# Front of an attention and gated feed-forward kernel: constants, load gates, queue order and the place of the scores

## The chip, the cores and the metric

The kernel runs on one core of one Trainium2 chip. The metric is the device time of one execution in microseconds (us), lower is better. Single-core executions here scatter by about 1 us; faster or slower needs 2%, which is 7.1 us. Every execution also has a mean granted TensorE clock: 1.0 is full speed, and one halved stretch of 3.4 us in some 355 us shows as 0.995. Where in the execution such a stretch lay is recorded for the profiled executions alone.

## The reference, cut to what matters

```
scores = scale * q @ k^T          # batch 8, heads 8, 576 positions, head size 64
mask   = window of 32 (heads 0-3) or 32 positions at stride 4 (heads 4-7), both causal
x      = softmax(scores + mask) @ v            -> 4608 tokens x 512
out    = (gelu(x @ w_gate) * (x @ w_val)) @ w_out      # 512 -> 1536 -> 512
```

All inputs and the output are float32 in HBM; the kernel computes in float16 with float32 sums.

## The kernel before

Tokens go through the feed-forward part in nine chunks of 512 columns. Attention of batch b is worked in between, as far as the next chunk needs it. Only the front has nothing to hide behind: q and k of batch 0 must land, be cast, transposed, scored, exponentiated and multiplied by v, before chunk 0 can start.

Words used below: w is w_gate and w_val together, loaded in thirds, each with a gate part and a value part. xT is the transposed output of attention. The first product multiplies xT by w; its sum over 512 is cut into four k slices, its 1536 result columns into twelve column blocks. The second product is by w_out, the output weights. The denominators are the sums of the softmax, the numerators its products with v. A gate, in the code, makes a DMA wait until another DMA has landed.

The parts that the change touches:

```python
def load_w(i):                      # a third of w_gate and one of w_val, GpSimd's queue (casts to f16)
    both = [nc.gpsimd.dma_start(out=t[i], in_=w[:, cs]...) for t, w in ((wg_t, moe_w_gate), (wv_t, moe_w_val))]
    gated(both[0])                  # waits for the DMA that gate["dma"] names, once
    return both
...
mask_plain()                        # GpSimd; VectorE then makes bias_p of mask_p, first thing after "ones"
gate_v = v_plain(0, sv0, nc.sync)   # five DMAs; the last one is returned
...
warm(30, 7)                         # 30 matmuls of ones, to bring the clock up
for vp_, _, vt_, _ in vset:         # constants, six memsets on VectorE
    nc.vector.memset(...)
for hp in range(2):                 # casts of q (VectorE) and k (ScalarE), batch 0
    ...
gate["dma"] = gate_v
load_w(0)
... scores of four head pairs, denominators ...
load_w(1)
copy("pool", tiles["v", 0][1], r4(first_vd))
wg2, _ = load_w(2)
...
num_split(0, 4)                     # ScalarE copies PSUM to SBUF, GpSimd multiplies into xT[0]
num_split(1, 0)                     # the same into xT[1]
...
gate["dma"] = wg2                   # q, k of batch 1 wait for it
... SyncE loads q, k of batch 1; GpSimd: dilated q, k of batch 1, output weights 0,
    then four casts of q, k, then output weights 1 and 2, dilated v ...
```

In chunk 0 the transposes of the cast q, k of batch 1 follow the column blocks 10 and 11 (`t_plain(1, q61, nb - 10, ...)`). The scores of batch 1 are laid between thirds of the second product (`ffn2`). GpSimd works its list strictly in order, so a DMA that it issues later starts later, and a cast that waits holds up everything behind it.

The softmax here doesn't subtract the row's maximum and nothing guards it: scores larger than these inputs give would overflow.

Of the kernel before, what the change touches and what calls it, by code (L numbers as in the profile page):

```python
# [21 lines left out]
def kernel(  # L22
# [100 lines left out]
    def mask_plain():  # L123
        nc.gpsimd.memset(mask_p, 1.0)
        band(mask_p[:, 0:PB].rearrange("p (r c) -> p r c", c=PW), 0, 0)
        band(mask_p[:, PB : PB + P].rearrange("p (r c) -> p r c", r=1), 0, 0)
        band(mask_p[:, PB + P : PH].rearrange("p (r c) -> p r c", r=1), 0, 64)
        nc.vector.tensor_scalar(bias_p, mask_p, 1.0, 60000.0, ALU.subtract, ALU.mult)

    def mask_dil():  # L130

# [5 lines left out]
    def load_w(i):  # L137
        cs = slice(i * CH, (i + 1) * CH)
        both = [
            nc.gpsimd.dma_start(out=t[i], in_=w[:, cs].rearrange("(kc p) n -> p kc n", p=P))  # L140
            for t, w in ((wg_t, moe_w_gate), (wv_t, moe_w_val))
        ]
        gated(both[0])
        return both
# [9 lines left out]
    def gated(ins):  # L154

        if "dma" in gate:
            tc.add_manual_dep(ins.ins, gate.pop("dma").ins.name, SYNC, reason="order of loads")
# [36 lines left out]
    def v_plain(b, sv, eng):  # L194
        for kb in range(5):
            k0 = min(kb * P, S - P)
            last = eng.dma_start(out=sv[:, kb], in_=v[b, 0:HK, k0 : k0 + P, :].rearrange("h p d -> p h d"))  # L197
            gated(last)
        return last

    def v_cast(b, sv):
        vp, vd, vt, vr = tiles["v", b]
# [37 lines left out]
    def load_v_dil(b):  # L240
        nc.gpsimd.dma_start(out=fl(tiles["v", b][1]), in_=quads(v, b, HK, 0, 4 * P))
        load_v_dil_rest(b)
# [53 lines left out]
    def cast_six(eng, q6, st, t, hp):  # L296

        h = slice(2 * hp, 2 * hp + 2)
        copy(eng, q6[:, t, :, h, :], st[:, t, h, :].rearrange("p h (r d) -> p r h d", r=6))
# [326 lines left out]
    def warm(n, bank):  # L626
        for _ in range(n):
            nc.tensor.matmul(ps[:, bank, :], ones[:, 0:P], ones, start=True, stop=True)


    for t, src, eng in ((0, q, nc.sync), (1, k, nc.scalar)):
        eng.dma_start(out=first_p[:, t], in_=sixes(src, 0))
# [11 lines left out]


    warm(30, 7)
    for vp_, _, vt_, _ in vset:
        nc.vector.memset(vp_.rearrange("p j g x d -> p (j g) x d")[:, :, 1, :], 1.0)
        nc.vector.memset(vt_[:, :, 1, :], 1.0)
    for hp in range(2):  # L650
        for t in range(2):
            cast_six(("dve", "act")[t], q6, first_p, t, hp)
    for hp in range(2):
        t_plain(0, q6, hp, 2 * hp, ("act", "dve"))
    nc.vector.tensor_scalar(bias_d, mask_d, 1.0, 60000.0, ALU.subtract, ALU.mult)
# [25 lines left out]
    t_dil(0, 1, qd0, 6, ("act", "act"))  # L681
    last_keys(0, 0, 2)
    last_keys(0, 2, HK, nc.gpsimd)
    load_w(1)
    copy("pool", tiles["v", 0][1], r4(first_vd))
    wg2, _ = load_w(2)

    dt0, dt1 = (den(n, -2 * n, t.rearrange("p (b c) -> p b c", c=32)) for n, t in enumerate(first_t))
    recip(0, dt0)
# [9 lines left out]
    num(3, 0)  # L699


    gate["dma"] = wg2
    st1 = ldp.tile([R6, 2, HK, 6 * D], F32, tag="st", name="st1")
    for t, src in ((0, q), (1, k)):
        gated(nc.sync.dma_start(out=st1[:, t], in_=sixes(src, 1)))
    sv1 = new_v(1)
    new_qt(1)
    qd1 = load_eights(1)
    load_wo(0)
    q61 = ldp.tile([R6, 2, 6, HK, D], F16, tag="qp", name="qp1")  # L710
    for hp in range(2):
        for t in range(2):
            cast_six("pool", q61, st1, t, hp)
    wo1 = load_wo(1)
    wo2 = load_wo(2)
    gate["dma"] = wo1
    v_plain(1, sv1, nc.sync)
    load_v_dil(1)
    v_cast(1, sv1)
    gate["dma"] = wo2  # L720
    tiles["plain", 2] = load_batch_plain(2)

    mm0 = 0
# [18 lines left out]
    for c in range(NCH):  # L742
        if 1 <= c and c + 2 < B:
            tiles["plain", c + 2] = load_batch_plain(c + 2)
            load_batch_rest(c + 2)
        pv_at = values_a.get(c, {})
        s_list = list(scores.get(c, ()))
        if c < 2:
            pairs = ((2, 3), (0, 1)) if c == 0 else ((0, 1), (2, 3))
        else:  # L750
            pairs = (ends, (mm0 + 1, mm0 + 2))
        SB = 4 - mm0

        masks = []
        pend = None
        for nb in range(NNB):
            if nb == 0 and c < 2:
                ffn1_two(c, ((4, 5), (6, 7)) if c == 0 else ((6, 7), (2, 3)), range(NKC), False)
            elif nb == 0 and late:
                ffn1_two(c, pairs, (2, 3, 0, 1) if c in (2, 3) else range(NKC), True)  # L760
            elif nb > 1 or not (c < 2 or late):
                ffn1(c, nb, pairs[nb % 2])
            if pend is not None:
                (norm_both_x if is_plain(pend) else norm_x)(pend, SB)
                pend = None
            if nb in pv_at:
                pend = pv_at[nb]
                if is_plain(pend):
                    emit_both(pend, SB)
                    norm_both_r(pend, SB)  # L770
                else:
                    emit_pv(pend, SB, wide=True)
                    norm_r(pend, SB, wide=True)
            if c == 0 and nb > 9:
                t_plain(1, q61, nb - 10, 4 + 2 * (nb - 10), ("act", "dve"))
            if nb == NNB - 1 and c > 0 and s_list:
                n = s_list.pop(0)
                masks.append(emit_s(n, SB, pe_mask=n in biased))

        def s_next():  # L780
            if s_list:
                n = s_list.pop(0)
                masks.append(emit_s(n, SB, pe_mask=n in biased))

        def mask_next():
            mask = masks.pop(0) if masks else None
            if mask is not None:
                mask()


        if c == 0:
            load_batch_rest(2)

            def third(i):
                for tb in range(2):
                    ffn2(c, tb, 2 + tb, fcs=range(4 * i, 4 * i + 4))
                    if i == 2:
                        store(c, tb, 2 + tb, "act")

            def s_of(n):  # L800
                mask = emit_s(n, 4, pe_mask=n > 5)
                if mask is not None:
                    masks.append(mask)


            s_of(4)
            t_dil(1, 0, qd1, 2, ("dve", "dve"))
            t_dil(1, 1, qd1, 0, ("dve", "dve"))
            last_keys(1, 0, HK)
            mask_next()  # L810
            third(0)
            s_of(5)
            den(4, -2)
            third(1)
            mask_next()
            s_of(6)
            den(5, -2)
            third(2)
            s_of(7)
            ffn2(c, 2, 2, {3: [lambda: den(6, -2)], 9: [lambda: num(4, 4)]})  # L820
            store(c, 2, 2, "act")
            ffn2(c, 3, 3, {0: [lambda: den(7, -2)], 4: [lambda: num(5, 6)]})
            store(c, 3, 3, "act")
            num(6, 0)
            num(7, 4)
            gelu_table()
        else:
            todo = list(values_b.get(c, ()))
            lone = c in values_b

            ends = (0, 3) if c == 1 else ends
            going = []

            def do(kind, tb):
                if kind == "s":
                    s_next()
                elif kind == "m":
                    mask_next()
                elif kind == "x":
                    norm_x(*going.pop(0))  # L840
                elif kind == "v":
                    n, flip = todo.pop(0), ends[tb % 2] != mm0
                    bank = mm0 + 1 - flip
                    emit_pv(n, bank, flip=flip)
                    norm_r(n, bank, flip=flip)
                    going.append((n, bank, flip))
                else:
                    n = todo.pop(0)
                    emit_pv(n, SB)
                    norm_parts(n, SB, min(S, (c + 2) * CH - n // NHP * S))  # L850

            for tb in range(4):
                at = [(fc, kind) for t, fc, kind in places.get(c, ()) if t == tb]
                hooks = {}
                for fc, kind in at:
                    if fc < NNB:
                        hooks.setdefault(fc, []).append(lambda kind=kind, tb=tb: do(kind, tb))
                bank = ends[tb % 2] if lone else mm0 + tb
                ffn2(c, tb, bank, hooks)
                store(c, tb, bank, "dve" if c > 5 and tb == 3 else "act")  # L860
                for fc, kind in at:
                    if fc == NNB:
                        do(kind, tb)
            if lone:
                gelu_table()

            late = lone and len(values_b[c]) > 2
            if c == 3:
                mm0 = 4 - mm0
            if c == 3 or not lone:  # L870
                ends = (mm0, mm0 + 3)
            while masks:
                mask_next()
# [28 lines left out]
```

## Time and profile before

| | before |
|---|---|
| time, median of 3 runs (lowest, highest) | 356.04 us (355.39, 356.18) |
| span of the profiled execution | 354.9 us, mean clock 0.995 |
| TensorE busy | 339.6 us, 96% |
| first product of chunk 0, its second k slice | 24.18 us, 25.54 us |
| first product of chunk 1 | 68.13 us |

TensorE is the engine with the most work, so its idle time is all that a reordering can win. The table of stretches, the chain of waits and the lists of GpSimd and TensorE are shown in the prediction. GpSimd's list: its columns are start, length, engine, line, operation, count, and in brackets the idle time before and what ended it.

```profile
41.06 0.82 POOL L292 CAST qp<-st 96x768 f16<-96x768 f32 x1 [13.37 <-DMA st<-in_q_dram]
44.18 2.37 POOL L292 CAST qp<-st 96x768 f16<-96x768 f32 x3 [2.30 <-DMA st<-in_k_dram]
```

These are the casts of q, k of batch 1 in the kernel before: GpSimd waits for q until 41.06 and for k until 44.18, so the first cast k is ready at 45.0. TensorE's transposes of them start at 45.33, without a wait, six of q and then six of k:

```profile
45.33 0.68 PE L305 MATMUL ps<-ident,qp 96*128 96x96 f16 x12
```

### The profile page before, as it was taken

Reading aid. Unit: us, or ns where it says so; the run is one execution under the profiler, and the core shown is the slowest. Engines: PE = TensorE matmul, PEld = TensorE weight load, DVE = VectorE, ACT = ScalarE, POOL = GpSimd, SP = SyncE. Lnnn points to the kernel's source line nnn. Section 1 sums busy time; section 2 is a strip of 40 time slices with the busy share of each in tenths; the row PEclk is TensorE's granted clock in tenths of the full one; section 3 lists DMA queues with packets and bytes.
Section 4 is the critical chain, followed back from the end, with each engine's and each line's share of the span. In section 5 each row is a group of like instructions: output and inputs, shape, how many; then the busy total and the mean of one; then the engine's idle time right before and its main releaser. Section 6 shows DMA issues by size and latency. Waiting matters only on the chain.

```text
span 354.9 us, 5997 instructions
## 1 busy us (share of the span) xinstructions
PE 339.6 (96%) x2338; PEld 164.0 (46%) x2338; DVE 201.9 (57%) x307; ACT 147.7 (42%) x219; POOL 81.4 (23%) x121
## 2 busy tenths in 40 slices
PE   8869999999999999999999999999999999999995
PEld 3534454444444444444545454544454444444442
DVE  1793466743486448873778756995499414403320
ACT  1653355343553364535462448235732223323321
POOL 8391161353143153063004400240000000000000
PEclk9998999999999999999999999999999999999999
DMA  8999969999999999799148962791200020020002
GB/s 178 174 197 205 210 98 206 181 155 180 235 175 161 237 162 168 196 173 152 61 125 187 136 125 77 180 172 50 88 2 0 31 89 1 2 81 37 2 30 89
DMA packets 106316, 44.44 MB, mean 125 GB/s; under 512 B 83280, under 2 KB 101584, under 8 KB 106288
## 3 DMA queue, kind: packets, MB, share of 16 engines
q1 hardware_dynamic: 84192, 31.14, 39.1%
q0 software_dynamic: 21696, 12.33, 27.7%
q10 hardware_dynamic: 400, 0.59, 0.7%
q8 instruction: 18, 0.29, 0.4%
q14 instruction: 10, 0.08, 0.1%
HBM read 39.85 MB, written 9.44 MB: 139 GB/s over the span
## 4 chain that ended last, share of the span: by engine, by line
PE 74%; DVE 10%; DMA 6%; issue 3%; POOL 2%; SPq 2%; ACT 1%; DVEq 0%; POOLq 0%; ACTq 0%
PE ps L575 46%; PE ps L609 21%; PE ps L463 4%; DMA sv<-in_v_dram 3%; DMA qTd<-rd 2%; DVE u_all L598 2%; DMA out_dram<-osb 2%; DVE dt L491 2%; DVE xT L501 1%; SPq L197 1%; PE ps L381 1%; DVE P L391 1%; POOL xT L676 1%; DVE qTd L294 1%; PE ps L351 1%
## 5 line engine op out<-in xcount | busy, mean ns | idle before, releaser
L598 DVE SCALAR_TENSOR_TENSOR u_all<-g,ps 128x512 f16<-128x512 f16 x108 | 72.8, 683 | 78.7 <-PE ps L575 71.5
L575 PE MATMUL ps<-xT,wg 128*128 128x512 f16 x432 | 115.0, 382 | 2.2 <-POOL xT L676 1.9
L597 ACT ACTIVATE g<-ps 128x512 f16<-128x512 f32 x108 | 63.9, 596 | 125.1 <-PE ps L575 124.6
L575 PE MATMUL ps<-xT,wv 128*128 128x512 f16 x432 | 114.8, 381 | 0.5 <-ACT osb L620 0.3
L609 PE MATMUL ps<-wo,u_all 128*128 128x512 f16 x432 | 99.8, 380 | 0.1
L575 PEld LDWEIGHTS <-wv 128*128 128x128 f16 x432 | 42.4, 98 | 54.7 <-issue 3.5
L575 PEld LDWEIGHTS <-wg 128*128 128x128 f16 x432 | 41.5, 98 | 49.5 <-issue 2.4
L609 PEld LDWEIGHTS <-u_all 128*128 128x128 f16 x432 | 39.6, 98 | 45.8 <-issue 0.7
L620 ACT ACTIVATE osb<-ps 128x512 f32<-128x512 f32 x33 | 19.7, 597 | 39.7 <-PE ps L609 39.2
L219 POOL CAST qp<-st 128x2048 f16<-128x2048 f32 x6 | 11.4, 1894 | 97.2 <-DMA st<-in_k_dram 57.2
L535 DVE STREAM_TRANSPOSE rb<-rc 128x576 f32<-128x576 f32 (+4 forms) x34 | 25.3, 743 | 1.3
L524 DVE STREAM_TRANSPOSE dt<-ps 128x576 f32<-128x576 f32 x21 | 16.3, 777 | 15.1 <-PE ps L463 15.1
L383 ACT ACTIVATE P<-ps 128x1152 f16<-128x1152 f32 x16 | 18.1, 1130 | 14.2 <-PE ps L381 13.5
L361 ACT ACTIVATE P<-ps 128x960 f16<-128x960 f32 x16 | 15.5, 970 | 12.2 <-PE ps L351 12.2
L550 DVE TENSOR_TENSOR xT<-ps,rb 128x576 f16<-128x576 f32 x16 | 17.9, 1127 | 1.4 <-PE ps L463 1.1
L622 DVE TENSOR_SCALAR osb<-ps 128x512 f32<-128x512 f32 x3 | 2.1, 692 | 27.8 <-PE ps L609 27.8
L463 PE MATMUL ps<-P,ones 128*64 128x96 f16 (+5 forms) x162 | 11.1, 249 | 3.9 <-DVE P L391 2.8
L391 DVE TENSOR_TENSOR P<-P,mask_d 128x1152 f16<-128x1152 f16 x11 | 8.3, 755 | 10.2 <-ACT P L383 10.2
L391 DVE TENSOR_TENSOR P<-P,mask_p 128x1344 f16<-128x1344 f16 x14 | 12.3, 887 | 2.6 <-ACT P L362 2.5
L463 PEld LDWEIGHTS <-ones 128*64 128x64 f16 x162 | 7.2, 108 | 12.7 <-issue 8.1
L491 DVE STREAM_TRANSPOSE dt<-ps 64x576 f32<-64x576 f32 x14 | 10.9, 780 | 0.4
L203 POOL CAST vp<-sv 128x1024 f16<-128x1024 f32 x8 | 8.6, 1076 | 10.5 <-DMA sv<-in_v_dram 10.5
(82 smaller groups left out, 243.9 us busy)
## 6 DMA issues: line engine op xcount, KB each, us to landing
out_dram<-osb SPq DMA_DIRECT2D x36, 256.0 KB, 2.0
sv<-in_v_dram SPq DMA_DIRECT2D x40, 128.0 KB, 3.7
st<-in_q_dram SPq DMA_DIRECT2D x24, 128.0 KB, 4.1
st<-in_k_dram SPq DMA_DIRECT2D x24, 128.0 KB, 3.2
vd<-in_v_dram POOLq DMA_DIRECT2D x7, 256.0 KB, 6.8
wg<-in_moe_w_gate_dram POOLq DMA_DIRECT2D x3, 512.0 KB, 7.6
wv<-in_moe_w_val_dram POOLq DMA_DIRECT2D x3, 512.0 KB, 9.5
wo<-in_moe_w_out_dram POOLq DMA_DIRECT2D x3, 512.0 KB, 8.4
```

Source lines behind the costliest of these rows:

```text
L383: nc.scalar.activation(pt, ps[:, b0 : b0 + 4, 0:DW], AF.Exp, bias=0.0, scale=scale)
L391: nc.vector.tensor_tensor(pt, pt, mb, ALU.mult)
L463: nc.tensor.matmul(o, lhs, rhs, start=st, stop=True, skip_group_check=True)
L491: nc.vector.transpose(dt[64 * hl : 64 * hl + 64].rearrange("p b c -> p (b c)"), both_rows(1 - hl, b0, hl))
L524: nc.vector.transpose(dst, den)
L535: nc.vector.transpose(rb[:, 0 : 32 * nb].rearrange("p (b c) -> p b c", c=32), bass.AP(tensor=rc.tensor, offset=rc.offset, ap=[rc.ap[0], [1 ...
L550: nc.vector.tensor_tensor(dst.rearrange("p (i m s) -> p i m s", m=2, s=2), num, rb.rearrange("p (s m i) -> p i m s", s=2, m=2), ALU.mult,)
L575: nc.tensor.matmul(ps[:, bank, :], w[:, kc, ns], xT[kc][:, tok], start=first, stop=end)
L597: nc.scalar.activation(g, ps[:, banks[0], :], AF.Gelu)
L598: nc.vector.scalar_tensor_tensor(u_all[:, nb, :], g, USCALE, ps[:, banks[1], :], ALU.mult, ALU.mult)
L609: nc.tensor.matmul(ps[:, bank, :], u_all[:, fc, tb * P : (tb + 1) * P], wo_t[fc // 4][:, fc % 4, :], start=(fc == 0), stop=(fc == NNB - 1),)
L620: nc.scalar.activation(osb, ps[:, bank, :], AF.Copy, bias=0.0, scale=1.0 / USCALE)
```

## The change

It is meant to shorten the front by about its idle time: constants before anything is needed, w let in earlier, w's last third issued behind the multiplications that the first product waits for, batch 1's loads in time for the earlier chunk 0, and the scores of batch 1 placed so that their masks are ready.

```diff
-        nc.vector.tensor_scalar(bias_p, mask_p, ...)            # in mask_plain
...
-            last = eng.dma_start(out=sv[:, kb], ...)
+            ins = eng.dma_start(out=sv[:, kb], ...)
+            if kb == 3:
+                fourth = ins                                    # returned: gate of w
...
+    for vp_, _, vt_, _ in vset:                                 # moved up, ahead of the first loads
+        nc.vector.memset(...)
...
+    nc.vector.tensor_scalar(bias_p, mask_p, ...)                # now behind the casts of q
...
-    load_w(1)
+    w1 = load_w(1)[1]
     copy("pool", tiles["v", 0][1], r4(first_vd))
-    wg2, _ = load_w(2)
... num_split(0, 4), num_split(1, 0), num(3, 0) ...
-    gate["dma"] = wg2
+    load_w(2)
+    gate["dma"] = w1
...
-    load_wo(0)
+    wo1 = [load_wo(i) for i in range(3)][1]
+    load_v_dil(1)
     ... four casts of q, k of batch 1 on GpSimd ...
-    wo1 = load_wo(1)
-    wo2 = load_wo(2)
     gate["dma"] = wo1
     v_plain(1, sv1, nc.sync)
-    load_v_dil(1)
-    gate["dma"] = wo2                                          # gate of batch 2's first loads: gone
... chunk 0: thirds of ffn2 per token block, so that one lies on each side of s_of(5) ...
-            t_dil(1, 1, qd1, 0, ("dve", "dve"))
+            t_dil(1, 1, qd1, 0, ("act", "dve"))
+            mask_next()
             last_keys(1, 0, HK)
-            mask_next()
-            third(0); s_of(5); den(4, -2); third(1); mask_next(); s_of(6); den(5, -2); third(2); s_of(7)
+            third(0, 0); s_of(5); third(1, 0); den(4, -2); mask_next(); s_of(6)
+            third(0, 1); third(1, 1); den(5, -2); s_of(7); third(0, 2); den(6, -2); third(1, 2)
```

(The calls of the last two groups stand one to a line in the kernel. Not shown: den and num calls inside the last two blocks of ffn2 move forward too.)

More of the change, by code (lines that the diff above doesn't have):

```diff
@@ L127, in mask_plain @@
         band(mask_p[:, PB + P : PH].rearrange("p (r c) -> p r c", r=1), 0, 64)
-        nc.vector.tensor_scalar(bias_p, mask_p, 1.0, 60000.0, ALU.subtract, ALU.mult)
     def mask_dil():
@@ L196, in v_plain @@
             k0 = min(kb * P, S - P)
-            last = eng.dma_start(out=sv[:, kb], in_=v[b, 0:HK, k0 : k0 + P, :].rearrange("h p d -> p h d"))
-            gated(last)
-        return last
+            ins = eng.dma_start(out=sv[:, kb], in_=v[b, 0:HK, k0 : k0 + P, :].rearrange("h p d -> p h d"))
+            gated(ins)
+            if kb == 3:
+                fourth = ins
+        return fourth
     def v_cast(b, sv):
@@ L628, in warm @@
             nc.tensor.matmul(ps[:, bank, :], ones[:, 0:P], ones, start=True, stop=True)
+    for vp_, _, vt_, _ in vset:
+        nc.vector.memset(vp_.rearrange("p j g x d -> p (j g) x d")[:, :, 1, :], 1.0)
+        nc.vector.memset(vt_[:, :, 1, :], 1.0)
     for t, src, eng in ((0, q, nc.sync), (1, k, nc.scalar)):
@@ L646 @@
     warm(30, 7)
-    for vp_, _, vt_, _ in vset:
-        nc.vector.memset(vp_.rearrange("p j g x d -> p (j g) x d")[:, :, 1, :], 1.0)
-        nc.vector.memset(vt_[:, :, 1, :], 1.0)
     for hp in range(2):
@@ L652 @@
             cast_six(("dve", "act")[t], q6, first_p, t, hp)
+    nc.vector.tensor_scalar(bias_p, mask_p, 1.0, 60000.0, ALU.subtract, ALU.mult)
     for hp in range(2):
@@ L792, with third @@
             load_batch_rest(2)
-            def third(i):
-                for tb in range(2):
-                    ffn2(c, tb, 2 + tb, fcs=range(4 * i, 4 * i + 4))
-                    if i == 2:
-                        store(c, tb, 2 + tb, "act")
+            def third(tb, i):
+                ffn2(c, tb, 2 + tb, fcs=range(4 * i, 4 * i + 4))
+                if i == 2:
+                    store(c, tb, 2 + tb, "act")
             def s_of(n):
@@ L807 @@
             t_dil(1, 0, qd1, 2, ("dve", "dve"))
-            t_dil(1, 1, qd1, 0, ("dve", "dve"))
+            t_dil(1, 1, qd1, 0, ("act", "dve"))
+            mask_next()
             last_keys(1, 0, HK)
-            mask_next()
-            third(0)
+            third(0, 0)
             s_of(5)
+            third(1, 0)
             den(4, -2)
-            third(1)
             mask_next()
             s_of(6)
+            third(0, 1)
+            third(1, 1)
             den(5, -2)
-            third(2)
             s_of(7)
-            ffn2(c, 2, 2, {3: [lambda: den(6, -2)], 9: [lambda: num(4, 4)]})
+            third(0, 2)
+            den(6, -2)
+            third(1, 2)
+            ffn2(c, 2, 2, {3: [lambda: num(4, 4)], 8: [lambda: den(7, -2)]})
             store(c, 2, 2, "act")
-            ffn2(c, 3, 3, {0: [lambda: den(7, -2)], 4: [lambda: num(5, 6)]})
+            ffn2(c, 3, 3, {2: [lambda: num(5, 6)]})
             store(c, 3, 3, "act")
```

## The prediction

> **What bounds the kernel now.** I read the page first (TensorE busy 96% of the 354.9 us span), then the table of stretches, to see where the other 4% lies.
>
> ```profile
> core 0: us, PE busy (x) PEld busy (x) DVE busy (x) ACT busy (x) POOL busy (x), PEclk, DMA share, GB/s
> 0.00:10.00 10.00, 8.37 (x30) 3.27 (x30) 2.10 (x6) 2.63 (x3) 8.11 (x23) 1.00 0.89 179
> 10.00:25.50 15.50, 10.62 (x184) 7.66 (x185) 13.42 (x25) 9.78 (x14) 9.98 (x13) 1.00 1.08 184
> 25.50:48.20 22.70, 22.66 (x117) 10.48 (x117) 9.13 (x14) 7.87 (x14) 7.04 (x10) 0.92 0.93 173
> 48.20:68.10 19.90, 18.46 (x198) 9.62 (x196) 14.33 (x24) 9.05 (x12) 5.63 (x9) 1.00 1.15 183
> ```
>
> The second column is the length, then each engine's busy time. TensorE stands still 4.9 us between 10 and 25.5 us (attention of batch 0) and 1.4 us between 48.2 and 68.1 us (attention of batch 1 beside the second product of chunk 0). Behind 69 us the waits of TensorE sum to 2.8 us in 286, so what is won before 68 us is kept, unless a load turns late. The change touches only the time before 68 us.
>
> Next the chain of waits around the first stretch's end:
>
> ```profile
> 5.84 9.39 DMA sv<-in_v_dram
> 15.23 0.29 issue
> 15.52 0.43 POOL wg L140
> ...
> 20.24 1.06 POOL vd L292
> ...
> 22.70 2.79 POOL xT L676 x2
> 25.50 0.04 issue
> 25.54 0.59 PE ps L575
> ```
>
> Columns: start, length, what. The end of the front is set by GpSimd, not by TensorE: v's fifth part lands at 15.23, then GpSimd issues and casts without a pause until it multiplies xT twice, and only then does the first product (L575) run on. Between 21.29 and 22.70 on it lie the two issues of w's last third. Its list:
>
> ```profile
> 21.21 0.75 POOL L140 DMA_DIRECT2D wg<-in_moe_w_gate_dram  x1
> 21.95 0.76 POOL L140 DMA_DIRECT2D wv<-in_moe_w_val_dram  x1
> 22.70 2.79 POOL L676 TENSOR_TENSOR xT<-xT,rb 128x576 f16<-128x576 f32 x2
> ```
>
> And TensorE's:
>
> ```profile
> 24.18 0.38 PE L575 MATMUL ps<-xT,wg 128*128 128x512 f16 x1 [1.62 <-POOL xT L676]
> ...
> 25.54 0.59 PE L575 MATMUL ps<-xT,wg 128*128 128x512 f16 x1 [0.33 <-POOL xT L676]
> 25.92 0.63 PE L575 MATMUL ps<-xT,wv 128*128 128x512 f16 x1
> ...
> 28.90 0.40 PE L575 MATMUL ps<-xT,wg 128*128 128x512 f16 x1
> 53.87 0.48 PE L463 MATMUL ps<-P,ones 128*64 128x512 f16 x6 [0.80 <-DVE P L391]
> ```
>
> The first four products start 0.216 us apart from 24.18, the next eight (25.54 to 28.90) 0.42 us apart, then 0.216 again: eight matmuls cost 1.7 us more than they would. The last line is the wait of the second stretch: denominators of head pair 4 wait 0.80 us for its mask on VectorE.
>
> **What the Trainium skill says.** "TensorE: Matmul & The Clock Gate", Part 1: an idle window of about 3.4 us halves the clock, the window runs free, and the halving lasts until a busy one has passed. The trace agrees: granted clock 0.5 from 25.52 for 3.413 us, after a window in which TensorE was busy 1.65 of 3.4 us. "DMA: Bandwidth & Descriptors", Queues, rings and completion order: the DMA engines take the queues' packets in turn. The trace agrees in part: batch 1's q, issued by SyncE at 32.43, shows packets only from 36 us while the GpSimd queue still streams w; afterwards the two share. "SBUF — State Buffer", SBUF: two separate sides: VectorE in a two-port mode keeps GpSimd from writing descriptors. No line of this trace isolates that; I keep it as a risk of the moved constants.
>
> **The change part by part.**
>
> *Constants first.* VectorE sits until 8.28 (6.81 us for the mask), writes bias_p (0.44) and six constants (8.77 to 10.69), and only then casts q, which landed at 7.97. TensorE's transposes, free from 9.90, start at 11.23. After: constants from 1.5 to 3.5 us, casts at about 8.05 to 9.0, bias_p to 9.5. ScalarE's k casts (from 8.65, end 10.21) suffice. Transposes start at 9.9: the attention chain moves 1.3 us forward (first scores at 11.6 for 12.93; q, k of the dilated heads landed at 11.81 and 13.04, needed at about 13.1 and 13.4). It does not move the front's end by 1.3, because GpSimd is not in this chain.
>
> *Gate.* v's fourth part lands at 15.00, the fifth at 15.23 (the landings in the trace): 0.23 us.
>
> *w's last third behind the multiplications.* Takes 1.51 us (0.75 and 0.76) off GpSimd before L676. With the gate: 22.70 - 0.23 - 1.51 = 20.96. The multiplication also needs ScalarE's copies (20.74 to 22.05). Their chain gains less than 1.3, since pair 3's scores need GpSimd's copy of keys (now 18.43, then 18.2 to 18.6): exponent 3 at 19.05 for 19.71, copies end about 20.7 and 21.4. So xT 0 is ready at 22.4 and xT 1 at 23.8, for 24.1 and 25.5: 1.7 us.
>
> *But the weights.* The first wv part lands 7.57 us after its issue at 16.29, at 23.86. From 17 us on nothing else streams (about 205 GB/s), so it can come only 0.23 sooner: 23.63. TensorE then begins wv at 23.65; four products of the first k slice end at 24.5, the second slice follows at once (xT 1 was there at 23.8). Before, the second slice began at 25.54. Gain: 25.54 - 24.5 = 1.0 us, at equal clock. VectorE's parts 2 and 3 of xT (before 24.00 to 26.13) come some 0.2 sooner and are needed at 25.4 and 26.2: just in time.
>
> *Clock.* TensorE's idle time before the products shrinks from 1.62 + about 0.5 us to about 1.4 in one piece, nearer the kind of window (8.45 to 11.87, with 1.33 idle) that did not throttle. I give three chances in four that the 1.7 us is then saved. But before does not pay it in every run either: the profiled run (356.65) did; the timed runs are 355.39 to 356.18, so I estimate 1.1 of the 1.7 as paid on average. After pays 0.25 x 1.7 = 0.4. Gain 0.7.
>
> *q, k of batch 1 after w's second third, output weights ahead of the casts.* The gate opens at about 28.7 (wv 1 landed at 28.96) in place of 32.4. Counting 3.5 us until its packets flow and the 145 GB/s it had at first, q lands at about 36.3 and k at 40.3 (41.0 and 44.1 before). GpSimd's issue of the last v part waits for a semaphore lane that w's last part frees (about 36), then the casts run: 37 to 43 for 41.06 to 46.55. TensorE wants the first k cast at about 42.7, has it at 41.2. No gain by itself; it keeps the front's gain from being lost. Batch 1's v lands near 54 for 61, which allows num(4) earlier.
>
> *Scores closer.* After the first scores of batch 1: three of four dilated copies on VectorE (0.69 each), then the mask (0.83) before last_keys (0.29): mask end 53.82 less 0.69 and 0.29 = 52.85 on before's clock. TensorE has the same eight products and one score block in between and arrives at about 52.95. The 0.80 wait goes; the next scores then wait some 0.1 to 0.2 for the exponent, as they follow the denominators directly. Gain 0.7.
>
> Sum: 1.0 + 0.7 + 0.7 = 2.4. 356.04 - 2.4 = 353.7 us.
>
> **Rivals.** (1) The front's full 1.7 us comes, or more, if the first weights land earlier than I think; against it: the DMA engines are full from 17 us. It would make 353. (2) The loads collide: with 2.5 MB of output weights, v and dilated q, k queued behind w's last third, and q, k of batch 1 let in sooner, w's last third or the k cast comes late and TensorE stops between 37 and 45 us. For it: the margins are 1.5 us (k cast) and 2 us (wv 2, wanted near 38.3, landing near 36 instead of 35.18). Against it: total bytes are equal and GpSimd's list now holds nothing else. It would give back 1 to 2 us: 355 to 356. (3) The clock falls to half again: 354.6 to 355. (4) The early constants hold up GpSimd's first loads (1.4 to 4.25 us), dilated q, k land after 13.4 and the attention loses its lead: about 354.2, since the weights bind anyway.
>
> **Range and chances.** The sure parts (1.0 and 0.7) give 354.3 with the clock unchanged; with everything good 352.4; a collision or cold clock 355.3. Range 352.3 to 355.3. Over 2% would need 7.1 us, more than all idle time of the touched stretches (6.3 us), so faster by 2% has 1 in 100; slower by 2% would need a new stop of 7 us that no margin suggests: 1 in 100.
>
> **What would show it.** First transposes at 9.9; w's issue at 15.3; GpSimd's L676 from about 21; the first L575 matmul at 22.4 with TensorE then waiting for wv until 23.65; no run of 0.42 us matmuls; q casts on GpSimd from about 37 without TensorE waiting at L305; no 0.8 us at the denominators of pair 4; the second chunk's first product at about 64.7 for 68.13 with the clock full, 66.4 with it halved. It is wrong if wv's first part lands off 23.6 by more than 0.5 us, if TensorE shows a wait over 0.5 us between 26 and 48, or if a DMA wait appears behind 68.

## The result, and the profile after

| | before | after |
|---|---|---|
| median us (lowest, highest), 4 runs each | 355.78 (355.39, 356.18) | 353.64 (353.20, 354.37) |
| ratio, 95% interval | | 0.9942 (0.9920, 0.9964) |
| span, mean clock of the profiled execution | 354.9, 0.995 | 351.5, 1.0 |

A ratio here is the mean time of one kernel's fast runs over the mean of the other's of the same rounds, so it is not quite the ratio of the medians. The gain is 2.1 us, 0.6%; at the 2% threshold the two count as the same.

The table of stretches of the changed kernel (length, busy time of TensorE, weight loads, VectorE, ScalarE, GpSimd, then clock):

```profile
10.00:25.50 15.50, 12.67 (x195) 8.52 (x194) 12.40 (x20) 9.57 (x13) 10.59 (x16) 1.00 1.10 187
25.50:45.80 20.30, 19.80 (x112) 9.44 (x111) 8.78 (x14) 7.85 (x14) 8.68 (x12) 1.00 1.21 222
45.80:65.10 19.30, 18.62 (x198) 9.34 (x196) 13.71 (x23) 9.49 (x13) 4.17 (x7) 1.00 1.11 192
```

TensorE's idle time in the first fell from 4.9 to 2.8 us, in the last (scores of batch 1 up to chunk 1) from 1.4 to 0.7. The middle stretch now has 0.5 us of idle time that it did not have.

The chain of waits of the changed kernel, around the place where the front used to end:

```profile
19.08 10.66 DMA wv<-in_moe_w_val_dram
...
30.17 12.08 DMA st<-in_k_dram
42.26 0.05 issue
42.31 0.83 POOL qp L293
43.14 0.05 issue
43.19 0.43 PE ps L306 x6
```

The chain no longer passes through GpSimd's multiplications and the first product. It goes from w's second third straight to k of batch 1 (its landing opens k's gate), to the cast, to the transposes. GpSimd's list and TensorE's list of the changed kernel, in the same columns as before:

```profile
21.04 2.76 POOL L679 TENSOR_TENSOR xT<-xT,rb 128x576 f16<-128x576 f32 x2 [0.16 <-ACT xT L678]
23.74 0.80 POOL L139 DMA_DIRECT2D wg<-in_moe_w_gate_dram  x1
...
38.40 0.82 POOL L293 CAST qp<-st 96x768 f16<-96x768 f32 x1 [1.67 <-DMA st<-in_q_dram]
42.31 2.36 POOL L293 CAST qp<-st 96x768 f16<-96x768 f32 x3 [3.09 <-DMA st<-in_k_dram]
```

```profile
22.50 0.38 PE L576 MATMUL ps<-xT,wg 128*128 128x512 f16 x1 [0.35 <-POOL xT L679]
23.48 0.39 PE L576 MATMUL ps<-xT,wv 128*128 128x512 f16 x1 [0.61 <-DMA wv<-in_moe_w_val_dram]
23.70 0.38 PE L576 MATMUL ps<-xT,wg 128*128 128x512 f16 x1
...
43.19 0.43 PE L306 MATMUL ps<-ident,qp 96*128 96x96 f16 x6 [0.50 <-POOL qp L293]
```

The first product starts 1.7 us sooner, then TensorE waits for w's first value part as forecast, and no product is slow. New is the last line: TensorE waits 0.50 us for the cast k of batch 1.

The 3.4 us between the two profiled executions split by three starts in TensorE's lists (third column block of chunk 0, first scores of batch 1, first product of chunk 1):

| | before | after | gained in this part |
|---|---|---|---|
| third column block starts | 29.79 | 26.73 | 3.06, of which 1.7 is the halved clock of the before execution |
| first scores of batch 1 start | 48.18 | 45.79 | -0.67 (18.39 became 19.06) |
| chunk 1 starts | 68.13 | 65.12 | 0.62 (19.95 became 19.33) |
| end of span | 354.9 | 351.5 | 0.4 |

The last 0.4 lies at one wait behind 68 us: a group of denominators waited 0.75 us for a mask at 102.79 before, and 0.24 us at 99.27 after. The prediction did not count it. The repeat has 0.22 us there, and d_only below, whose edit is one gate, 0.23; no run tests the cause.

The timed gain is only 2.1 us. The experiments had to say why.

### The profile page after: what moved, and what is told of

Its sections match the earlier page's. It is cut to its first block, busy times and chain, and to the rows that moved or that the text cites. A ratio compares the mean times of both kernels' runs of the same rounds, so it can differ in the third digit from the quotient of the medians.

```text
span 351.5 us, 5997 instructions
## 1 busy us (share of the span) xinstructions
PE 339.0 (96%) x2338; PEld 163.5 (47%) x2338; DVE 201.2 (57%) x306; ACT 148.2 (42%) x220; POOL 82.1 (23%) x121
## 4 chain that ended last, share of the span: by engine, by line
PE 71%; DVE 12%; DMA 10%; issue 3%; POOL 1%; ACT 1%; SPq 1%; DVEq 0%; ACTq 0%
PE ps L576 41%; PE ps L610 22%; PE ps L464 4%; DMA st<-in_k_dram 3%; DMA sv<-in_v_dram 3%; DMA wv<-in_moe_w_val_dram 3%; DVE u_all L599 2%; DVE dt L492 2%; DVE rb L536 1%; DVE dt L525 1%; DVE xT L551 1%; DVE xT L502 1%; DVE P L392 1%; PE ps L382 1%; PE ps L352 1%
## 5 line engine op out<-in xcount | busy, mean ns | idle before, releaser
L536 DVE STREAM_TRANSPOSE rb<-rc 128x576 f32<-128x576 f32 (+4 forms) x34 | 25.3, 743 | 1.3
L247 POOL DMA_DIRECT2D vr<-in_v_dram x16 | 10.0, 633 | 4.7 <-DMA wv<-in_moe_w_val_dram 3.1
```

Source lines behind the costliest of these rows:

```text
L536: nc.vector.transpose(rb[:, 0 : 32 * nb].rearrange("p (b c) -> p b c", c=32), bass.AP(tensor=rc.tensor, offset=rc.offset, ap=[rc.ap[0], [1 ...
```

## The experiments

Twelve kernels ran, each with five rounds against the kernel before; all gave correct results. "Changed" below is the changed kernel. Ratios are to the kernel before; 0.001 is 0.36 us. The later calls ran on other chips, so runs of different calls are compared by their ratios; the kernel before itself averaged 355.93, 355.93 and 356.02 us in the three.

**after_again: changed, unedited, as the yardstick.**

> The changed kernel once more, as the yardstick of this set. Expected: ratio to before 0.994 (0.9925 to 0.996), that is about 2 us less. If the profiled execution has a stretch of halved clock it is longer by up to 1.7 us than one without; in one without, the second chunk's first product starts at about 65.1 us.

Median 353.34 (353.21 to 354.43), ratio 0.9935 (0.9922 to 0.9948), that is 2.3 us. Chunk 1 starts at 65.54; the profiled execution, all at full clock from 4.77 on, waits 0.82 us for the cast k, as k landed at 42.69.

This call and the two later ones also gave 33 runs of the kernel before with their clocks. In 21 of them the mean clock was at most 0.995: mean time 356.01 us. In 12 it was at least 0.998: 355.87 us (355.96 and 355.88 in the 22 runs before d_only). **In the kernel before, the halved clock costs 0.14 us (95% interval -0.08 to 0.36), not 1.7.** That contradicts a term of the prediction, and the loads of batch 1 became the suspect.

**u_qkgate: changed, q and k of batch 1 let in by w's last third again.**

```diff
-    load_w(2)
-    gate["dma"] = w1
+    gate["dma"] = load_w(2)[0]
```

> The changed kernel, but q, k of batch 1 are let in by w's last third, gate part, as before, in place of w's second third. Theory: that gate opens at about 32.1 for 29.74; k lands about 2.4 us later (44.7 for 42.26), and TensorE, which wants the first cast k at 42.7, waits about 2.9 us at the transposes of batch 1 in place of 0.5: loss 2.4 us. Rival: with q, k let in later w's last third and dilated q, k come sooner and q, k catch up when the queue is empty: loss under 0.7 us.

Median 355.58 (355.05 to 356.92), ratio 0.9990 (0.9978 to 1.0002): nearly all of the gain is gone. TensorE's list and GpSimd's in this run:

```profile
45.33 0.43 PE L306 MATMUL ps<-ident,qp 96*128 96x96 f16 x6 [2.77 <-POOL qp L293]
```

```profile
44.45 2.37 POOL L293 CAST qp<-st 96x768 f16<-96x768 f32 x3 [2.60 <-DMA st<-in_k_dram]
```

The front was as fast as in the changed kernel (third column block at 26.60), and TensorE then stood still for 2.77 us until k was cast, at the same time as in the kernel before. The profiled execution also fell to half clock right after this wait (45.79 to 49.21). So a faster front is worth next to nothing while k lands at 44.4. The first theory holds, and its size (2.4) roughly: 2.0 us by the difference of the two ratios, give or take 0.6. The 0.4 us that is left of the gain is about what the new place of the scores is worth (u_scores below).

**d_only: the kernel before with only that gate moved.**

```diff
-    load_w(1)
+    w1 = load_w(1)[1]
...
-    gate["dma"] = wg2
+    gate["dma"] = w1
```

> The kernel before with one edit: q, k of batch 1 let in by w's second third (value part) in place of its last third. Theory, formed after the first eight runs: in the kernel before the landing of k of batch 1 (44.13, cast by 45.0) bounds TensorE, so that a front at full clock gains nothing over one at half clock. Here k lands at about 42, cast by 42.9, while TensorE wants it at 45.6 with the halved clock in the front and at about 43.9 without: runs with halved clock stay at before's time, runs at full clock are 1.2 to 1.5 us shorter, two groups. Rival: k did not bind the kernel before; then nothing is gained and there are no two groups.

Ratio 0.9986 (0.9969 to 1.0003), and two groups, as expected: 354.56 and 354.57 us at clock 1.0; 355.51, 355.76, 356.10 and 356.33 at 0.993 to 0.995, mean 355.93. They differ by 1.36 us. The profiled execution is one of the first group; GpSimd's list, then TensorE's:

```profile
42.25 2.37 POOL L292 CAST qp<-st 96x768 f16<-96x768 f32 x3 [3.79 <-DMA st<-in_k_dram]
```

```profile
43.69 0.68 PE L305 MATMUL ps<-ident,qp 96*128 96x96 f16 x12
```

k is cast from 42.25, and the transposes run at 43.69 without a wait. In the kernel before they could not start sooner than the first cast k, 45.0, however fast the front was. With k early, the clock of the front shows in the time; with k late, it is hidden. The rival, that k did not bind the kernel before, falls: the first group has two executions only, but both are 0.9 us below the fastest of the 33 of the kernel before (355.46).

**u_w2: changed, w's last third issued before the multiplications again.**

```diff
     copy("pool", tiles["v", 0][1], r4(first_vd))
+    load_w(2)
...
-    load_w(2)
```

> The changed kernel with w's last third issued before GpSimd's multiplications again. Theory: two issues of 0.75 us delay both multiplications; second xT part ready at about 25.2 for 23.8, so the second k slice starts 1.1 us later (25.3 for 24.14), and the gap may let the clock fall to half again: loss 1.1 us, 2.8 with the clock. Rival: the landing of w binds, and the loss is under 0.3 us.

Median 354.48 (353.10 to 355.81), ratio 0.9959 (0.9937 to 0.9980). Two groups again: four runs at clock 0.993 or 0.994, mean 355.02, and two at 1.0, mean 353.25, which equals the changed kernel. TensorE's list of the profiled execution, one of the second group:

```profile
23.47 0.38 PE L576 MATMUL ps<-xT,wg 128*128 128x512 f16 x1 [1.62 <-POOL xT L679]
...
24.83 0.38 PE L576 MATMUL ps<-xT,wg 128*128 128x512 f16 x1 [0.33 <-POOL xT L679]
```

The second k slice starts at 24.83, 0.7 us later than in the changed kernel (24.14), where I had expected 1.1; v had landed 0.3 sooner in this run. In exchange w's second third landed at 28.36 for 29.74, k at 41.40 for 42.26, and the wait at the transposes is gone. So the two runs at full clock show no loss where I had expected 1.1 us; with v earlier by chance in the profiled one, a smaller loss is not excluded. The worth of the move seems to be the clock: the 1.62 us of idle time in one piece is back, and with it a low clock in four of six executions (one of nine of the changed kernel, in the first comparison and the repeat), at 1.8 us each. The counts are small, and the profiled execution had the 1.62 us too and kept its clock.

**u_const: changed, constants and bias_p written where they were.**

```diff
     warm(30, 7)
+    nc.vector.tensor_scalar(bias_p, mask_p, ...)
+    for vp_, _, vt_, _ in vset: ...      # and both taken away above
```

> The changed kernel with the constants and bias_p written where they were before (ahead of the q casts). Theory: the front is bound by the landing of w's first value part (23.4 us), so the attention chain's lead hides and the loss is only what VectorE's last xT parts (end 25.71 now, needed at 25.86) come late: transposes start about 0.5 later, loss 0.2 to 0.5 us. Rival: the attention chain bounds the front, and the loss is the whole shift of the transposes, 0.5 to 1.3 us, or the constants are worth nothing at all (0).

Median 353.76 (353.45 to 356.24), ratio 0.9958 (0.9935 to 0.9981), against 0.9935 of the yardstick: the intervals overlap, so the time does not decide. The trace says more. The transposes start at 11.25 for 10.68 and 9.60, but GpSimd's multiplications do not move:

```profile
20.99 2.76 POOL L678 TENSOR_TENSOR xT<-xT,rb 128x576 f16<-128x576 f32 x2 [0.20 <-ACT xT L677]
```

and the second k slice waits for w's value part, which happened to land at 23.91. The lead of the attention chain does not reach the front's end. That agrees with the theory; the loss it allowed (0.2 to 0.5 us) is neither shown nor excluded.

**u_scores: changed, the old order in chunk 0.**

```diff
-            third(0, 0); s_of(5); third(1, 0); den(4, -2); ...
+            third(0); s_of(5); den(4, -2); third(1); ...      # and the copies and masks as before
```

> The changed kernel with the old order of scores, masks and products in chunk 0. Theory: the wait of the denominators for pair 4's mask comes back (0.8 us at that row), loss 0.6 us (0.4 to 0.9), seen between the first plain scores of batch 1 and the second chunk's first product (19.33 us now, 19.95 before). Rival: the earlier landing of v already took that wait, loss 0.

Median 354.18 (353.72 to 354.36), ratio 0.9949 (0.9937 to 0.9961), 0.5 us over the yardstick; the intervals overlap, so the time alone does not show it. The trace does: the wait is back,

```profile
51.78 0.48 PE L464 MATMUL ps<-P,ones 128*64 128x512 f16 x6 [0.80 <-DVE P L392]
```

and from the first scores to chunk 1 it takes 20.01 us (46.10 to 66.11) for 19.32 in the yardstick: 0.69 us.

**u_wo: changed, output weights 1 and 2 and the dilated v behind the casts.**

```diff
-    wo1 = [load_wo(i) for i in range(3)][1]
-    load_v_dil(1)
+    load_wo(0)
...
+    wo1 = [load_wo(i) for i in (1, 2)][0]      # behind the casts; load_v_dil(1) behind v_plain
```

> The changed kernel with output weights 1 and 2 and the dilated v issued behind the casts again. Theory: while q, k of batch 1 stream, GpSimd's queue is as long up to about 45 us either way (w's rest, dilated q, k, output weights 0), so k lands at most 0.5 to 1 us sooner; the 0.5 us wait at the transposes shrinks or goes. Against that v of batch 1 is let in at about 50 us for 47.6 and its cast ends at about 58.5 or later, where pair 4's numerators want it at 58.4: they wait 0 to 1.5 us. Net between -0.5 and +1 us. Rival: the output weights ahead of the casts are only in the way of k, and undoing them gains 0.5 us or more.

Median 354.58 (354.34 to 355.24), ratio 0.9966 (0.9954 to 0.9978), 1.1 us over the yardstick. k landed no sooner (42.34), the wait at the transposes stayed (0.77), and v came late:

```profile
59.61 0.45 PE L464 MATMUL ps<-P,vp 128*64 128x160 f16 x8 [1.06 <-POOL vp L204]
```

So queuing the output weights and the dilated v ahead does not visibly hold k up, and it is what lets v in early enough for the scores' new place. A caution for all readings of k: in the seven profiles that share the changed kernel's gates of w and of q, k (changed, after_again, u_const, u_scores, u_wo, c_wgfirst, c_split), k landed anywhere from 42.26 to 43.59, so differences of about 1 us between two single profiles are scatter.

**g_third: changed, w let in by v's third part.**

```diff
-            if kb == 3:
+            if kb == 2:
```

> The changed kernel with w let in by v's third part (landed at 13.10) in place of the fourth (14.87). Theory: the empty DMA stretch of 15.5 to 17.5 us is filled, w's first value part lands 1.3 to 1.7 us sooner (about 22), the first product starts at about 22; but VectorE, busy without a pause from 14.4 to 25.7, delivers the last xT part at about the same time, and TensorE then waits for it at the fourth k slice: gain only 0.1 to 0.4 us. Rival: only w's landing bound the front, gain 1.0 to 1.5 us. Third: v's last parts and the dilated v come late by sharing, and GpSimd's casts with them: loss.

Median 352.46 (351.87 to 352.87), ratio 0.9902 (0.9889 to 0.9915), 1.2 us under the yardstick. My theory fell: VectorE's last xT part was not fixed at 25.7 but came at 24.36, because GpSimd's copies and casts, on which scores and numerators wait, moved forward too. w's first value part landed at 22.72, only 0.7 sooner. The size is that of the rival, but the profile does not give its whole cause: the third column block starts 0.7 to 0.8 sooner than in the two profiles of the changed kernel, k landed at 41.85 (42.26, 42.69), and chunk 1 starts 0.4 and 0.8 sooner. What share of the timed 1.2 us is k's and what w's stays open.

**g_wg1: changed, q and k of batch 1 let in by the gate part of w's second third.**

```diff
-    w1 = load_w(1)[1]
+    w1 = load_w(1)[0]
```

> The changed kernel with q, k of batch 1 let in by the gate part of w's second third (25.97) in place of its value part (29.74). Theory: k lands about 3 us sooner (39 for 42.26), the 0.5 us wait at the transposes of batch 1 goes; w's last value part lands at about 37.5 for 35.84, just before TensorE wants it at 37.96: gain 0.5 us. Rival: w's last part comes later than 38 and TensorE waits there instead: gain 0 or a loss up to 1 us.

Median 353.19 (352.90 to 353.66), ratio 0.9926 (0.9914 to 0.9938): no clear difference. k landed at 38.01 and the wait at the transposes is gone, but w's last value part landed at 38.30 for 35.84, and TensorE waits there instead:

```profile
38.34 0.82 PE L576 MATMUL ps<-xT,wv 128*128 128x512 f16 x3 [0.56 <-DMA wv<-in_moe_w_val_dram]
```

The rival was right. The two loads share the DMA engines, and one gate earlier only swaps the waits. (The line is from a window that ends at 39 us.)

**c_wgfirst: changed, gate products of two k slices before the value products.**

```diff
+        if c == 0:
+            for gi in range(2):
+                for kc in kcs[:2]:
+                    for nb in range(2):
+                        ffn1_part(c, nb, gi, pairs[nb][gi], [kc])
+            kcs = kcs[2:]
```

> The changed kernel, whose first two column blocks take all gate products of the first two k slices before the value products. Theory: TensorE works on gate parts while w's first value part is still landing; the third block starts 0.4 to 0.6 us sooner (26.2 for 26.8), so w's landing was what held the front. But k of batch 1 lands no sooner, so the wait at the transposes of batch 1 grows by as much (0.5 to 0.8 now, 1.0 to 1.4 then) and the time stays (within 0.2 us). Rival: the front alone sets the time, gain 0.5 us.

Median 353.68 (353.33 to 354.06), ratio 0.9936 (0.9923 to 0.9949): the time stays, but not by my reason. The third column block did not start sooner (26.80), since the gate products of the second slice waited 0.74 us for GpSimd's second multiplication, ready at 23.73. So xT's second part bounds the front just as closely as w's landing; the run cannot test what k hides. TensorE did wait 1.10 us for the cast k, as expected, but only because k landed at 42.93 in this profile.

**c_split: changed, transposes of batch 1 split by tensor.**

```diff
-    for hp in range(2):
-        for t in range(2):
+    for t in range(2):
+        for hp in range(2):
             cast_six("pool", q61, st1, t, hp)
...
-                t_plain(1, q61, nb - 10, 4 + 2 * (nb - 10), ("act", "dve"))     # head pair: q and k
+                t_half(1, q61, nb - 10, 4 + 2 * (nb - 10), ("act", "dve"))      # tensor: both head pairs
```

> The changed kernel with the transposes of batch 1 split by tensor in place of head pair: q (landed 4 us sooner) cast and transposed first, both pairs, k one column block (1.73 us) later. Theory: the wait for the cast k at the transposes (0.5 to 0.8 us) goes and the time falls by as much. Rival: the wait moves to the next place, pair 4's scores, which want the copied k; no gain.

Median 352.68 (352.21 to 355.20), ratio 0.9917 (0.9894 to 0.9940), 0.6 us under the yardstick (one of the six runs, at clock 0.989, took 355.20). k landed late in the profiled execution (43.59), yet TensorE waits only 0.20 us for it, one column block later. The gain is about the wait's size, but the intervals overlap, so it is not shown by the time.

**best_third: g_third, c_wgfirst and c_split together.**

> The changed kernel with w let in by v's third part, the gate products first, and the transposes split by tensor. If these add up: w's landing -0.7, gate products first -0.5, k's wait -0.8, so about 2.3 us less than the changed kernel, ratio to before 0.987 (0.985 to 0.989), second chunk's first product at about 63.3 us. If the loads of w and k bind whatever the order of products: 0.989 to 0.9905 only.

Median 351.46 (351.06 to 353.09), ratio 0.9878 (0.9860 to 0.9897): 4.3 us less than before, 2 us less than the changed kernel, the fastest of all and within the expected 0.985 to 0.989. Chunk 1 starts at 62.97 (63.3 expected). The chain of waits, asked from 28 us on, now runs along TensorE there, not along a load:

```profile
28.00 12.95 PE ps L591 x60
40.95 0.51 PE ps L321 x12
41.46 1.74 PE ps L591 x8
```

No wait for w's value part or for a cast k is left in TensorE's list.

## Why the prediction was right or wrong

The time was right: 353.7 us predicted, 353.64 measured, within the range. Its sum of 2.4 us (1.0 front, 0.7 clock, 0.7 scores) is close to the measured 2.1 and 2.3. But one of the three terms is wrong in its reason, and another step is where much of the gain is made. That the sum came out is partly luck: the 0.7 of the clock is not there, and the earlier k, which was counted as "no gain by itself", stands in its place. One of the prediction's own signs of being wrong was met as well: a TensorE wait over 0.5 us between 26 and 48 us. It is 0.50 in the first profile and 0.82 in the repeat, in the place that rival 2 named.

- **Constants first: right.** The transposes start at 10.68, not 9.9, as the 30 warming matmuls ran at half clock until 6.96 in this execution; at 9.60 in the repeat. That it "does not move the front's end by 1.3, because GpSimd is not in this chain" agrees with u_const's trace. Rival 4 did not come: GpSimd issues its first loads at 1.40, 2.29 and 3.00 us before and after.
- **Gate and w's last third: right.** xT 0 ready at 22.44 and xT 1 at 23.80, predicted 22.4 and 23.8.
- **"But the weights": right.** Landing of w's first value part 23.43, predicted 23.63; second slice 24.14, predicted 24.5. The profiles give 1.4 us for 1.0 at equal clock: about 0.2 because w landed sooner, and 0.2 because the first gate product ran while TensorE waited for it, which I had not counted. c_wgfirst adds that xT 1 is an equal bound.
- **Clock: the step that failed is "I estimate 1.1 of the 1.7 as paid on average. Gain 0.7".** The changed kernel does keep its clock (one of nine executions at most 0.995), and a low clock does go with 1.4 to 1.8 us where k is early (d_only, u_w2). But the kernel before hardly paid: 21 runs with it averaged 356.01 us and 12 without 355.87. I read the slow products off TensorE's list and did not ask whether TensorE would have waited for something else had they been fast. It would have: the first cast k came at 45.0, and at full clock TensorE wants it near 43.9 (d_only's transposes start at 43.69, the six of q first). The window was misread too: the 3.413 us right before the halving, 22.11 to 25.52, had TensorE busy 1.48 us; the 1.65 belongs to 21.9 to 25.3.
- **q, k of batch 1: half right.** "No gain by itself; it keeps the front's gain from being lost" is right in both halves for the changed kernel (u_qkgate). I did not see that the kernel before was already bound by it. k landed at 42.26, not 40.3, so the transposes waited 0.50 and 0.82 us, a small part of rival 2. Of these 2 us (landing of k), 1.0 is the gate (29.80 for 28.8) and 0.6 the longer landing (12.1 us from issue for the 11.5 that my figures imply); the rest is that k is issued 0.4 after q.
- **Scores closer: right.** 0.7 predicted; 0.62 between the profiles, 0.69 in the trace of u_scores and 0.5 (not clear of noise) in its time.
- **Behind 68: right.** No DMA wait of TensorE's matmuls appears there.

In place of the wrong term: in the kernel before, TensorE reaches the transposes of k at 45.0 at the earliest, and at 45.59 with a slow front. In the changed kernel it does at 43.19, or 43.62 in the repeat. That is 1.4 to 2.4 us, and the scores add 0.6; the sum, 2.0 to 3.0, holds the measured 2.1 and 2.3, but leaves out the 0.4 behind 68 us. This is worked out from the traces and agrees with u_qkgate and d_only; no trace of the kernel before at full clock was taken, so its wait for k is inferred and not seen. One thing does not fit: by 45.0 and 45.59 a run of the kernel before at full clock should still be some 0.5 us shorter than a halved one, and the measured 0.14 (at most 0.36) is less. Why stays open.

## What to carry to other kernels

Before you count a slow stretch as a cost, ask which load or cast comes next and when it will be there: time saved ahead of a late load is lost at that load. Two groups in the times that go with the granted clock, present in one version and absent in another, hint at whether the early part or the load binds. Move a load's gate together with the work ahead of it, and if one more step of the gate only swaps two waits (g_wg1), try the order of use instead (c_split, best_third).

## What the Trainium skill lacked or had wrong

- "TensorE: Matmul & The Clock Gate", Part 1, says that an idle window halves the clock, and that short idle times between bursts can make it swing; it gives no share of busy time. Counted in steps of 3.413 us from each profile's first change of the clock, the window before the halving here (before, 22.11 to 25.52) had 1.48 us busy, so a window need not be empty. Windows with 1.72 (d_only, 22.85 to 26.26), 1.77 (u_w2, 20.85 to 24.27) and 1.87 us (changed, 17.20 to 20.61) were not followed by a halving, but neither was one with 1.42 us near the end of the kernel before (349.78 to 353.19). So no threshold can be read from these runs.
- "DMA: Bandwidth & Descriptors", Queues, rings and completion order: packets are taken in turn, but the page does not say how long a new transfer takes to get its first turn while another queue streams (it gives a first-byte time, with no such load named). With GpSimd's queue streaming, q of batch 1 was issued at 32.43 and moved its first packets in the microsecond from 36 on; after the change issued at 29.80 and moving from 33 on. It is not that w must be through first: w's last part landed at 35.18 before, but at 35.84 after. The first q load of the kernel, with empty queues, was issued at 0.81 and moved in the microsecond from 1 on.
- "SBUF — State Buffer", SBUF: two separate sides, says that VectorE and GpSimd share a port pair, and that one of them can lock the other out of it; it gives no figure for the two instructions met here. These runs agree with it, without isolating it: GpSimd's six selects of the mask took 2.38 us where VectorE's casts of q came after them (before, d_only, u_const) and 2.93 and 2.89 us where the casts ran beside them (changed, repeat; 2.58 to 2.97 in the other runs of that kind).
- No page has it, and I could not settle it: the value part of w's second third landed 2.5 us after its gate part in the kernel before and in u_w2 (26.42 and 28.96; 25.80 and 28.36), but 3.8 us after it in the changed kernel (25.97 and 29.74), where w's last third is issued later. It opened k's gate that much later. The later issue cannot be all of it: g_third, which issues in the same order, has 2.6 us (25.26 and 27.85), best_third 3.2 (24.94 and 28.15).
